# Layer 2's token sums taken from GpSimd to TensorE, with a newly searched instruction order

## Chip, core, metric

One core of a Trainium2 chip runs the whole kernel. The time is that of the core on the device, in microseconds (us); medians are given over several executions, with the range in brackets. The span, from the first to the last instruction in the trace, is 1.7 to 2.1 us shorter than the time in the profiled executions. Each execution also has a mean granted TensorE clock (1.0 is full speed). All comparisons are between executions that the records call fast; a single look has no state of its own, and is used where its clock is 1.0.

## The reference

Four layers work on x of 2048 tokens by 512, in bf16: linear attention, feed-forward, and both once more.

```python
def _A_ref(x, wqkv, wo):                  # layers 0 and 2; 32 heads of 16
    q, k, v = ...(x @ wqkv)...
    phi = lambda t: where(t > 0, t + 1, exp(t)) + 1e-6
    pq, pk = phi(q), phi(k)
    kv  = einsum("bhsd,bhse->bhde", pk, v)
    z   = einsum("bhsd->bhd", pk)         # the token sums of pk
    num = einsum("bhqd,bhde->bhqe", pq, kv)
    den = einsum("bhqd,bhd->bhq", pq, z)[..., None] + 1e-6
    return reshape(num / den) @ wo
def _B_ref(x, w1, w2):                    # layers 1 and 3; inner width 1376
    return maximum(x @ w1, 0) @ w2

x = x + _A_ref(_layernorm(x), ...)        # and so on: A, B, A, B
```

The change concerns z, the sum of pk over all 2048 tokens, in layer 2.

## The kernel before

The kernel builds a graph of small operations, each with its engine, what it reads and what it writes. A table, found beforehand by a search in a model of durations, gives the order in which they are issued; a second gives the bank, one of eight, of PSUM (the memory that holds TensorE's results) for each tile. Operations that may run on two engines carry an `a` (ScalarE) or `d` (VectorE) in the table. The tokens are 16 tiles of 128, in four chunks of four tiles.

For each tile, TensorE projects k, ScalarE and VectorE make pk of it, and in layer 2 (`zpn[0]` is 3) GpSimd adds the pk of the first three chunks into one f32 tile, which it splits into a high and a low bf16 half:

```python
def a_k_proj(i):
    b = alloc_bank()
    mm_group(... Tb[:, i, c, :], wqkv[:, c, D:2 * D] ...)           # 4 matmuls of N = 512
    phi_evac(b, pk_tile(i), ...)                 # ScalarE lin, exp; VectorE em (L515), phi (L517)
    if 0 < i < 4 * zpn[0]:
        prev = pk_tile(0) if i == 1 else zacc
        g.add(POOL, lambda e: e.tensor_tensor(zacc, prev, pk_tile(i), ALU.add), ...)     # L588
        if i == 4 * zpn[0] - 1:
            g.add(POOL, lambda e: e.tensor_copy(zhl[:, 0, :], zacc), ...)                # L591
            g.add(POOL, lambda e: e.tensor_tensor(zhl[:, 1, :], zacc, zhl[:, 0, :], ALU.subtract), ...)
```

What GpSimd hasn't summed goes to TensorE, as matmuls with a column of ones: pk is the weight side, so one of them is a weight load of 128x128 and a single column. The tiles and the two halves gather in one PSUM bank:

```python
def a_z_acc(lo, hi, zb, first):      # i < 0: one of the two halves
    return [(psv[:, zb, j:j + 1], src(i, j), ones[:, 0:1], ...)
            for i in range(lo, hi) for j in range(4)]
def tail_z():
    if zpn[0]:
        a_z_acc(-2, 0, zb, True)                                    # 8 matmuls of N = 1
    for k in range(zpn[0], NCH):
        a_z_acc(4 * k, 4 * k + 4, zb, k == 0)                       # 16 per chunk
```

Between layers the chunk's row statistics are small VectorE instructions of 128x4, with one power on GpSimd; then a tile pair is normalised and transposed by a DMA from SBUF to SBUF, whose result the next projection reads:

```python
def ln_chunk(t, first):              # L452 nm2, L454 var, L456 veps, L458 rstd, L460 nbias
    g.add(DVE,  ... nm2[:, sl] ...)
    g.add(DVE,  ... var[:, sl] ...)
    g.add(DVE,  ... veps[:, sl] ...)
    g.add(POOL, ... rstd[:, sl] = veps ** -0.5 ...)
    g.add(DVE,  ... nbias[:, sl] ...)
def tr_dma(lo, hi):
    dma(lambda e: e.dma_start_transpose(Tb[:, lo:hi], xn[:, lo:hi]), ..., 550.0 * (hi - lo), ...)
```

## Time and profile before

| | before |
|---|---|
| time, median of 3 | 277.51 us (277.36 to 278.38) |
| the execution that was profiled | 278.55 us, span 276.7, clock 1.0 |
| TensorE: 1893 matmuls, issue time | 263.4 us |
| TensorE: sum of its real stalls in that execution | 2.95 us |

The page's share of TensorE can't be used for fine readings, as the ends of matmuls are modelled. The issue time is worked out from starts instead, with the undisturbed steps that the prediction gives (216 ns for 128x512). A stall is what a start comes later than such a step. At a change to or from the tiled matmuls of the denominators the next start comes some 0.1 us later; these steps, and three others of 0.11 to 0.14 us, are left out of the 2.95 (the 0.19 at 176 us contains one).

One more line, from the page's list of DMA issues, for the transposes; the last number is the median from issue to landing.

```profile
Tb<-xn SPq DMA_TRANSPOSE x30, 3.2
```

### The profile page before, as it was taken

What the parts mean: (1) busy time and instruction counts of PE and PEld (TensorE: products, weight loads), DVE (VectorE), ACT (ScalarE), POOL (GpSimd) and SP (SyncE); (2) the same over time, 40 slices, a digit from 0 to 9 for tenths busy, and PEclk for the clock granted to TensorE, in tenths of its full rate; (3) what the DMA queues carried; (4) which work ended last, traced back from release to release, by engine and by line L of the source; (5) the groups of instructions that cost most, each with busy time, mean ns of one, the idle gap of its engine ahead of it and who ended that gap; (6) DMA issues with size and microseconds to landing.
All of it is one profiled execution on the core that took longest, in us unless ns stands there. A gap on an engine that the chain in (4) does not pass through costs nothing.

```text
span 276.7 us, 5086 instructions
## 1 busy us (share of the span) xinstructions
PE 268.8 (97%) x1893; PEld 162.4 (59%) x1893; DVE 239.6 (87%) x604; ACT 193.6 (70%) x423; POOL 33.3 (12%) x43
## 2 busy tenths in 40 slices
PE   6999999999999999999999999999999999999995
PEld 2444454434356766778756444344447777988884
DVE  4999789998995988499899978999999878899885
ACT  4898846998866179388678668589986958845510
POOL 3111000000201010001143481000012010100000
PEclk9999999999999999999999999999999999999999
DMA  6946960040413024201402130000340120600014
GB/s 207 378 97 100 264 202 0 0 78 19 77 32 65 0 40 91 45 19 27 52 0 42 39 73 2 0 2 14 64 95 2 38 57 12 165 19 2 1 76 154
DMA packets 41976, 18.35 MB, mean 66 GB/s; under 512 B 36352, under 2 KB 40544, under 8 KB 41952
## 3 DMA queue, kind: packets, MB, share of 16 engines
q1 hardware_dynamic: 41808, 17.96, 27.4%
q8 instruction: 15, 0.25, 0.4%
q14 instruction: 9, 0.07, 0.1%
q10 hardware_dynamic: 144, 0.07, 0.1%
HBM read 7.01 MB, written 2.10 MB: 33 GB/s over the span
## 4 chain that ended last, share of the span: by engine, by line
PE 81%; DVE 8%; DMA 8%; ACT 2%; issue 1%; SPq 0%
PE ps L531 81%; DMA Tb<-xn 4%; DMA w<-in_B_w_dram 2%; DVE big L517 1%; DMA xin<-in_A_x_dram 1%; DVE xres L575 1%; DVE bst L438 1%; DVE escr L515 1%; DVE xres L943 1%; ACT xn L468 1%; DVE xres L544 0%; DVE veps L456 0%; DVE nbias L460 0%; DVE xn L470 0%; DVE wper L785 0%
## 5 line engine op out<-in xcount | busy, mean ns | idle before, releaser
L513 ACT ACTIVATE escr<-ps 128x512 bf16<-128x512 f32 x64 | 37.8, 608 | 10.3 <-PE ps L531 9.5
L511 ACT ACTIVATE big<-ps 128x512 bf16<-128x512 f32 x64 | 37.7, 609 | 4.5 <-PE ps L531 4.4
L531 PE MATMUL ps<-Tb,w 128*128 128x512 bf16 x160 | 38.2, 379 | 0.0
L538 ACT ACTIVATE sqscr<-xres 128x512 bf16<-128x512 f32 x48 | 29.9, 628 | 6.4 <-DVE xres L575 6.0
L531 PE MATMUL ps<-wqkv,Tb 128*128 128x512 bf16 x128 | 30.8, 379 | 1.7 <-ACT rstd L1009 1.1
L531 PE MATMUL ps<-Tb,wqkv 128*128 128x512 bf16 x128 | 30.9, 379 | 0.5 <-DVE gw L621 0.5
L531 PE MATMUL ps<-gw,big 128*128 128x512 bf16 x128 | 31.4, 380 | 0.0
L531 PE MATMUL ps<-big,xn 128*128 128x512 bf16 x128 | 30.7, 379 | 0.0
L517 DVE TENSOR_TENSOR big<-big,escr 128x512 bf16<-128x512 bf16 x64 | 28.1, 462 | 0.9
L531 PE MATMUL ps<-w,xin 128*128 128x256 bf16 x190 | 26.3, 273 | 0.0
L564 POOL TENSOR_TENSOR rstdf<-varf,nhalf 128x4 f32<-128x4 f32 x8 | 8.5, 1072 | 138.9 <-DVE varf L562 53.2
L531 PEld LDWEIGHTS ps<-Tb,w 128*128 128x128 bf16 x160 | 15.1, 98 | 16.3 <-issue 0.5
L741 ACT ACTIVATE big<-ps 128x512 bf16<-128x512 f32 x34 | 19.7, 595 | 6.2 <-PE ps L531 6.1
L948 ACT ACTIVATE ps<-ps 128x256 f32<-128x256 f32 x28 | 10.5, 374 | 18.7 <-PE ps L531 16.4
L515 DVE TENSOR_SCALAR escr<-escr 128x512 bf16<-128x512 bf16 x64 | 19.4, 315 | 4.2 <-ACT escr L513 4.1
L531 PE MATMUL ps<-w2s,big 128*128 128x256 bf16 x160 | 21.9, 273 | 0.4 <-DVE xres L943 0.4
L531 PEld LDWEIGHTS ps<-wqkv,Tb 128*128 128x128 bf16 x128 | 12.1, 97 | 15.9 <-ACT rstd L1009 1.5
L865 ACT ACTIVATE big<-ps 128x512 bf16<-128x512 f32 (+1 forms) x33 | 16.8, 519 | 6.5 <-PE ps L531 6.2
L531 PE MATMUL ps<-w,big 128*128 128x256 bf16 (+2 forms) x113 | 21.1, 302 | 0.0
L531 PEld LDWEIGHTS ps<-Tb,wqkv 128*128 128x128 bf16 x128 | 12.0, 98 | 15.4 <-DVE gw L621 0.8
L531 PEld LDWEIGHTS ps<-w,xin 128*128 128x128 bf16 x190 | 18.5, 98 | 4.1 <-DVE xn L976 0.2
L531 PEld LDWEIGHTS ps<-big,xn 128*128 128x128 bf16 x128 | 12.2, 98 | 14.5 <-issue 0.5
(145 smaller groups left out, 494.1 us busy)
## 6 DMA issues: line engine op xcount, KB each, us to landing
wqkv<-in_A_wqkv_dram SPq DMA_DIRECT2D x3, 512.0 KB, 7.1
xin<-in_A_x_dram SPq DMA_DIRECT2D x3, 512.0 KB, 8.0
out_dram<-xn SPq DMA_DIRECT2D x3, 512.0 KB, 2.7
w<-in_B_w_dram SPq DMA_DIRECT2D x1, 1376.0 KB, 6.8
w<-in_B_w_dram SPq DMA_DIRECT2D x1, 1280.0 KB, 9.9
wo<-in_A_wo_dram SPq DMA_DIRECT2D x1, 512.0 KB, 10.0
Tb<-xn SPq DMA_TRANSPOSE x30, 3.2
xin<-in_A_x_dram SPq DMA_DIRECT2D x1, 384.0 KB, 3.2
```

The costliest lines, as they stand in the source:

```text
L438: g.add(DVE, lambda e: e.bn_stats(bst[:, i, :], xin[:, i, :]), [("xin", i)] + list(behind), [("bst", i)], C_DVE_BNST, name="bnst%d" % i)
L468: alts = [(ACT, lambda e: e.activation(xn[:, i, :], src, ACTF.Identity, scale=rstd[:, i:i + 1], bias=nbias[:, i:i + 1]), C_ACT_SB_AP), (DV ...
L511: g.add(ACT, lambda e: e.activation(dst_ap, psv[:, b, :], ACTF.Identity, bias=1.0 + 1e-6, scale=1.0), [("ps", b)], [dst_key], C_ACT_PSUM, ...
L513: g.add(ACT, lambda e: e.activation(escr[:, s, :], psv[:, b, :], ACTF.Exp), [("ps", b)], [("escr", s)], C_ACT_EXP, name=name + "_exp")
L515: g.add(DVE, lambda e: e.tensor_scalar(escr[:, s, :], escr[:, s, :], 1.0, 1e-6, ALU.min, ALU.add), [("escr", s)], [("escr", s)], C_DVE_BF4 ...
L517: g.add(DVE, lambda e: e.tensor_tensor(dst_ap, dst_ap, escr[:, s, :], ALU.max), [dst_key, ("escr", s)], [dst_key], 340.0, name=name + "_phi")
L531: last = e.matmul(o, l, r, start=st, stop=sp, skip_group_check=skip)
L538: g.add(ACT, lambda e: e.activation(sqscr[:, q, :], xres[:, i, :], ACTF.Square, accum_out=dst[:, i:i + 1]), [("xres", i)], [("sqscr", q), ...
L564: g.add(POOL, lambda e: e.tensor_tensor(rstdf[:, sl], varf[:, sl], nhalf[:, 0:4], ALU.pow), [("varf", t), ("nhalf",)], [("rstdf", t)], C_P ...
L741: g.add_flex([(ACT, lambda e, M=M, b=b, u=u: e.activation(unit_ap(u, M), psv[0:M, b, :], ACTF.Relu), C_ACT_PSUM), (DVE, lambda e, M=M, b=b ...
L865: g.add_flex([(ACT, lambda e: e.activation(out_ap(r, m), pv(b), ACTF.Relu), cost(C_ACT_PSUM)), (DVE, lambda e: e.tensor_scalar(out_ap(r, m ...
L948: g.add_flex([(ACT, lambda e: e.activation(psv[:, c1, cols], psv[:, c2, L], ACTF.Identity), 290.0), (DVE, lambda e: e.tensor_copy(psv[:, c ...
```

## The change

The intent is to take the f32 sums off GpSimd, where they block VectorE, and to give the search two truer durations: the transposes and the landing of the k weights (`wk`). Both tables are new. The diff, cut:

```diff
 ORDER = """
-17 0 14 12 15 18 13 1 16 19 2 20 22 3 24 4 21 23 25 5 6 26 27 7 28 8 29 40 30 33 31 32a ...
+17 0 14 12 15 18 13 1 16 19 2 20 22 3 24 4 21 23 25 5 6 26 27 7 28 8 29 33 30 47 31 32a ...
 ... (some 50 lines, all changed)
-BANKS = ("01435143526072607607676767706207072602266007067670720702760672...
+BANKS = ("01364701325424652425454545452625426426525564646246455426544262...
-... DEN_PRE=1, LATE_A=1, ZP=(0, 3), WK_ACT=False, ...
+... DEN_PRE=1, LATE_A=1, ZP=(0, 0), WK_ACT=False, ...
-        dma(... wqkv[:, :, D:2 * D] ..., 1650.0, "ld_wk", ...)
+        dma(... wqkv[:, :, D:2 * D] ..., 2000.0, "ld_wk", ...)
-                ... 550.0 * (hi - lo), "tr%d" % lo, issue=C_SP_TR)
+                ... 750.0 * (hi - lo), "tr%d" % lo, issue=C_SP_TR)
```

The two durations serve the model alone; on the chip they act only through the tables found with them.

## The prediction

> **What bounds the kernel now.** I read the page first (shares, then the chain), then TensorE's timeline, then VectorE's and GpSimd's timelines around the places where TensorE stood still, then the instructions of single lines.
>
> The engine shares and the chain that ended last:
>
> ```profile
> PE 268.8 (97%) x1893; PEld 162.4 (59%) x1893; DVE 239.6 (87%) x604; ACT 193.6 (70%) x423; POOL 33.3 (12%) x43
> ...
> PE 81%; DVE 8%; DMA 8%; ACT 2%; issue 1%; SPq 0%
> ```
>
> TensorE is the bound, and 97% says there is hardly any idle time to win. But ends of matmuls are modelled, so I counted from the starts. In undisturbed runs a 128x512 matmul starts 216 ns after the last, a 128x256 one 109, a 128x128 one 55 to 58, a 128x1 one 25. Summed over 1893 matmuls that is 263.4 us of issue. TensorE starts at 1.2 us and ends at 273.9; the remaining 9.0 us are 3.6 us of start-up (mostly waiting for the first weights and normalised tiles), some 2.5 us of small steps, most of them where TensorE changes to and from the tiled denominator matmuls, and six real stalls: 0.30 us at 37 us, 0.91 at 61.5, 0.59 at 143.8, 0.44 at 152.2, 0.19 at 176.1 and 0.52 at 179.6. They sum to 2.95 us, about 1.1% of the time. This is all that a better order can win outside the head and the tail.
>
> Two of the six, on TensorE's timeline where layer 1 hands over to layer 2:
>
> ```profile
> 143.10 1.03 PE L531 MATMUL ps<-wqkv,Tb 128*128 128x512 bf16 x4
> 144.55 1.26 PE L531 MATMUL ps<-w2s,big 128*128 128x256 bf16 x10 [0.42 <-DVE xres L943]
> ...
> 150.67 1.89 PE L531 MATMUL ps<-big,xn 128*128 128x512 bf16 x8
> 152.84 1.04 PE L531 MATMUL ps<-wqkv,Tb 128*128 128x512 bf16 x4 [0.28 <-DMA Tb<-xn]
> ```
>
> Four matmuls from 143.10 are issued by 143.96, yet the next starts at 144.55: 0.59. Eight from 150.67 are issued by 152.40, the next starts at 152.84: 0.44. Why VectorE was late there is on its own timeline, beside GpSimd's:
>
> ```profile
> 142.56 1.15 DVE L456 TENSOR_SCALAR veps<-var 128x4 f32<-128x4 f32 x1
> 145.39 1.27 DVE L517 TENSOR_TENSOR big<-big,escr 128x512 bf16<-128x512 bf16 x1
> 146.92 1.06 DVE L460 SCALAR_TENSOR_TENSOR nbias<-mean,rstd 128x4 f32<-128x4 f32 x1
> ...
> 142.54 1.16 POOL L588 TENSOR_TENSOR lden<-lden,big 128x512 f32<-128x512 f32 x1 [2.45 <-DVE var L454]
> 145.23 1.15 POOL L588 TENSOR_TENSOR lden<-lden,big 128x512 f32<-128x512 f32 x1 [0.42 <-DVE big L517]
> 146.81 1.15 POOL L588 TENSOR_TENSOR lden<-lden,big 128x512 f32<-128x512 f32 x1 [0.42 <-DVE big L517]
> ```
>
> A 128x4 instruction takes 1.15 us, and each long one ends when a GpSimd addition ends. All executions of these lines:
>
> ```profile
> L456 DVE TENSOR_SCALAR veps<-var x4: 170/170/1151, 102.4 to 153.8; 128x4 f32<-128x4 f32 x4
> L517 DVE TENSOR_TENSOR big<-big,escr x64: 407/419/1378, 11.0 to 197.7; 128x512 bf16<-128x512 bf16 x64
> ```
>
> Minimum, median, maximum: 0.17 against 1.15 us, 0.42 against 1.38. So the f32 sums cost VectorE, not GpSimd, and through it the two stalls.
>
> **What the Trainium skill says.** (1) "SBUF — State Buffer", section "SBUF: two separate sides": VectorE and GpSimd share one port pair, held for a whole instruction, and the loser "fully blocks". The trace agrees: VectorE's long instructions end with the 1.15 us addition. (2) "TensorE: Matmul & The Clock Gate", section "Back-to-back issue gap": an isolated matmul steps by N/2.4 + 2.5 ns, but in a stream of weight load and matmul both set the step. At N = 512 the trace has the formula's 216 ns; at N = 1 it has 25 ns, not 3, so the second half decides, and I use 25. (3) "Perfetto Trace Analysis", section "Identifying the Most-Contended Engine", warns against matmul busy time as a measure; here it shows 268.8 us where 263.4 is the issue.
>
> **The change part by part.**
>
> *Removed:* in layer 2 eleven additions, one copy and one subtraction on GpSimd, 11.9 + 1.2 + 0.6 + 1.2 = 14.9 us of an engine that is 12% busy. Worth nothing by itself. On VectorE it removes the blocking. Seven cases I can name: veps 1.15 for 0.17, nm 1.12 for 0.16, nbias 1.06 and 1.11 for 0.15, three L517 at 1.27, 1.27 and 1.38 for 0.42. Together 6.5 us of VectorE time between 142 and 162 us, where it is 94% busy. On the path that ends the kernel only what reached TensorE counts: 0.59 + 0.44 = 1.03 us.
>
> *Added:* chunks 0 to 2 of layer 2 (12 tiles, 4 matmuls each) go to the matmul with ones, 48 matmuls; the 8 on the two GpSimd halves go. Net 40. On TensorE's timeline:
>
> ```profile
> 170.98 0.34 PE L531 MATMUL ps<-ones,rhi 128*128 128x1 bf16 x8
> 171.18 0.54 PE L531 MATMUL ps<-ones,big 128*128 128x1 bf16 x16
> 171.58 1.02 PE L531 MATMUL ps<-big,xn 128*128 128x512 bf16 x4
> ```
>
> Starts 170.98, 171.18 and 171.58: 8 in 0.20 us, 16 in 0.40, thus 25 ns each. 40 x 25 = 1.0 us, fully on the bound engine. So removal and addition by themselves cancel: -1.03 + 1.00 = 0.
>
> *Moved:* the whole order is new, made with a transposed pair taking 0.75 us per tile instead of 0.55 and the first weights 0.35 us later. Fixed parts of the kernel's own model aside, that lengthens a pair by 0.4 us; the page has 3.2 us from issue to landing as the median of 30, and the chain shows that some are much longer:
>
> ```profile
> 57.90 4.63 DMA Tb<-xn
> ...
> 149.56 3.23 DMA Tb<-xn
> ```
>
> The 4.63 us one caused the largest stall, 0.91 us at 61.5. In the new order I counted TensorE work between the last matmul that feeds this transpose and the first that needs it: 6.8 us instead of 6.4, and the centring that precedes it moves ahead of the evictions. I expect 0.3 us to remain of 0.91. The stall at 37 us (sums waiting for pk of the last tiles) has one group of four 0.22 us matmuls put between in the new order; 0.1 of 0.30 remains. At 176 to 180 us, TensorE waits for the reciprocal chain and then for a PSUM bank that VectorE evicts after the last accumulation of G. The new order still lets 0.36 us of work stand between that accumulation and the first user of the bank, and the reciprocal has 3.0 us of TensorE work behind which to hide, while it took about 3.2 (two ScalarE passes of 0.69 and 0.63, a copy and a product of 0.42 and 0.75 on VectorE, plus gaps). So 0.5 of 0.71 stays. The head keeps its first projection at 7.2 us, since the first weights land at 7.0; nothing in the change makes them land earlier.
>
> Sum: stalls 2.95 - (0.3 + 0.1 + 0.5) = 2.05 us won, 1.0 us added, -1.05 net. A new order also makes new stalls; the old one left 1.9 us of stalls that no GpSimd sum explains, and a search with longer transposes should leave fewer. I allow 0.05 us beyond the 0.9 kept, little because the VectorE time won also helps other evictions: 277.5 - 1.05 + 0.05 = 276.5.
>
> **The rivals.** *A: only the added matmuls are felt.* The VectorE time won lies beside TensorE work, and the new order has its own stalls of the old size. Then 277.5 + 1.0 = 278.5 at most. For it: 268.8 of 276.7 us busy, and only 1.03 us of stalls are tied to GpSimd. Against it: both stalls are tied directly, link by link. *B: all stalls vanish.* 277.5 - 2.95 + 1.0 = 275.6; a shorter head or tail could take it to 275. For it: the search is told of the transposes that were too short. Against it: the G eviction has the same 0.36 us of cover. *C: a transpose becomes the new wait.* At the start of layer 2 the first transposed pair of chunk 2 has 10.8 us of TensorE work between producer and consumer, against 12.6 in the old order. Residuals, the row statistics with weight differences of 0.82 us put between them, the 1.03 us power, normalising and 3.2 us of transfer use some 10.5. A transfer of 4.6 us there would cost about 1.1 us: 277.6.
>
> **Range and chances.** The centre is 276.5. B bounds it below at 275.2 with a little from head and tail; C, or A in half, bounds it above at 277.9. A gain over 2% needs 272.0, less than the sum of issue, head and tail allows (even without any stall 275 or so): 0.01. A loss over 2% needs 283.1, five times the added matmuls; only a badly misjudged wait in the new order could do it: 0.02. Within 2%: 0.97.
>
> **What would show it right or wrong.** In the changed profile GpSimd should lose L588, L591 and L592, nothing else, and fall from 33.3 to about 18 us busy; L456, L452 and L460 should have maxima near 0.2 us and L517 near 0.45; 128x1 matmuls should number 128 and still step by 25 ns; the matmul issue should sum to 264.4. TensorE should show no wait on L943 or on a transpose between 138 and 155 us. The prediction is wrong if VectorE's long cases vanish but the stalls at the layer change persist (then the sums were not their cause), if a transpose wait over 0.5 us stands at the start of layer 2 (C), or if new stalls elsewhere sum to over 2 us.

## The result

The changed kernel takes 277.32 us (277.22 to 277.49, 4 runs) against 277.72 (277.36 to 278.38, 4 runs) of the kernel before in the same rounds. The ratio is 0.9983, with a 95% interval of 0.9962 to 1.0005. Ratios here are the mean time of one kernel's fast runs over that of the other's of the same rounds, so not quite the ratio of the medians quoted. The time is inside the range of 275.2 to 277.9, and "within 2%" was right. But the gain that was forecast, about 1.0 us, came out at 0.4 us by these medians and 0.17% (0.5 us) by the ratio; a repetition below gives 0.06 us. Where the rest went is the question.

The shares and the chain that ended last, of the changed kernel:

```profile
PE 268.6 (97%) x1909; PEld 164.2 (60%) x1933; DVE 236.8 (86%) x617; ACT 190.1 (69%) x410; POOL 18.3 (7%) x30
...
PE 94%; DVE 4%; issue 1%; ACT 0%; DVEq 0%
```

GpSimd has 13 instructions and 15 us less. DMA has left the chain, where it had 8%. 1933 weight loads are 40 more, as planned; the 1909 matmuls are fewer than the loads only because some records are missing (a second trace of this kernel, taken below, has all 1933).

Two of the lines that had been blocked, with minimum, median and maximum in ns:

```profile
L456 DVE TENSOR_SCALAR veps<-var x4: 164/170/171, 106.9 to 150.8; 128x4 f32<-128x4 f32 x4
```

```profile
L517 DVE TENSOR_TENSOR big<-big,escr x64: 409/424/428, 9.2 to 195.0; 128x512 bf16<-128x512 bf16 x64
```

The maxima were 1151 and 1378 ns; now no instruction of these lines is far from its median. TensorE's timeline at the hand-over from layer 1 to layer 2 (start in us, modelled duration, engine, line, operation, what, how many):

```profile
140.29 1.02 PE L531 MATMUL ps<-wqkv,Tb 128*128 128x512 bf16 x4
141.40 0.72 PE L531 MATMUL ps<-w2s,xin 128*128 128x256 bf16 x5
...
148.06 1.89 PE L531 MATMUL ps<-big,xn 128*128 128x512 bf16 x8
149.78 2.75 PE L531 MATMUL ps<-wqkv,Tb 128*128 128x512 bf16 x11
```

The first transposed chunk is used at 149.78 without a wait: eight matmuls from 148.06 at 0.216 us each end their issue at 149.79. The wait on a residual isn't quite gone: four from 140.29 are issued by 141.15, and the next starts 0.25 us later. The view names no cause for it; VectorE's timeline has two residual sums (L943) that end at 141.34, 0.06 us before that start. Further on, two waits persist, and there is a new one in the last layer:

```profile
178.36 0.40 PE L531 MATMUL ps<-rsp,esel 32*128 32x512 bf16 x4
179.14 2.12 PE L531 MATMUL ps<-Tb,wqkv 128*128 128x512 bf16 x9 [0.38 <-DVE gw L621]
```

```profile
266.23 0.71 PE L531 MATMUL ps<-w2s,big 128*128 128x256 bf16 x5
267.12 0.72 PE L531 MATMUL ps<-w2s,escr 128*128 128x256 bf16 x5 [0.18 <-DVE xres L943]
```

Five matmuls of 256 columns take 0.55 us to issue, so from 266.23 the next could start at 266.78, and starts 0.34 us later.

| TensorE's stalls, us, at | before, first profile | changed |
|---|---|---|
| 37 | 0.30 | 0 |
| 61 | 0.91 | 0 |
| 141 to 144 (residual) | 0.59 | 0.25 |
| 149 to 152 (transpose) | 0.44 | 0 |
| 176 to 180 | 0.19 + 0.52 | 0.17 + 0.44 |
| 267 | 0 | 0.34 |
| sum | 2.95 | 1.20 |
| issue time | 263.4 | 264.4 |

On this table the stalls fall by 1.75 and the issue rises by 1.0. The two traces' spans, 276.7 and 275.5, even fall by 1.2; the other 0.4 us lie mostly in the start-up and in the three small steps, which the new order doesn't have. This looks like the prediction come true, and it is deceptive: the first of the two executions was not a usual one.

### The profile page after: what moved, and what is told of

Same layout as the page of the kernel before. It is cut to its first block, busy times and chain, and to the rows that moved or that the text cites. A ratio compares the mean times of both kernels' runs of the same rounds, so it can differ in the third digit from the quotient of the medians.

```text
span 275.5 us, 5131 instructions
## 1 busy us (share of the span) xinstructions
PE 268.6 (97%) x1909; PEld 164.2 (60%) x1933; DVE 236.8 (86%) x617; ACT 190.1 (69%) x410; POOL 18.3 (7%) x30
## 4 chain that ended last, share of the span: by engine, by line
PE 94%; DVE 4%; issue 1%; ACT 0%; DVEq 0%
PE ps L531 92%; PE ps L415 2%; DVE xn L571 1%; DVE xres L575 1%; DVE xres L943 1%; PE ps L494 0%; DVE gw L621 0%; ACT Tb L501 0%; DVE xn L976 0%; DVE Tb L502 0%; DVE ps L949 0%; DVEq L1240 0%; DVE wrm L408 0%; ACT lnv L1007 0%
## 5 line engine op out<-in xcount | busy, mean ns | idle before, releaser
L531 PE MATMUL ps<-wqkv,Tb 128*128 128x512 bf16 x121 | 30.0, 379 | 0.7 <-DVE Tb L502 0.3
L531 PE MATMUL ps<-Tb,wqkv 128*128 128x512 bf16 x128 | 30.3, 379 | 0.4 <-DVE gw L621 0.4
L531 PE MATMUL ps<-gw,big 128*128 128x512 bf16 x118 | 29.4, 379 | 0.7 <-issue 0.2
L531 PE MATMUL ps<-big,xn 128*128 128x512 bf16 x123 | 29.7, 379 | 0.4 <-issue 0.2
L517 DVE TENSOR_TENSOR big<-big,escr 128x512 bf16<-128x512 bf16 x64 | 26.2, 423 | 2.9 <-ACT big L511 1.5
L515 DVE TENSOR_SCALAR escr<-escr 128x512 bf16<-128x512 bf16 x64 | 17.8, 289 | 9.8 <-ACT escr L513 9.4
L531 PEld LDWEIGHTS ps<-w,xin 128*128 128x128 bf16 x190 | 18.3, 98 | 4.7 <-DVE ps L949 0.3
L698 DVE TENSOR_TENSOR big<-big,ps 128x512 bf16<-128x512 bf16 x32 | 20.3, 682 | 0.4 <-PE ps L531 0.2
```

Of the source, the lines that this page charges most:

```text
L515: g.add(DVE, lambda e: e.tensor_scalar(escr[:, s, :], escr[:, s, :], 1.0, 1e-6, ALU.min, ALU.add), [("escr", s)], [("escr", s)], C_DVE_BF4 ...
L517: g.add(DVE, lambda e: e.tensor_tensor(dst_ap, dst_ap, escr[:, s, :], ALU.max), [dst_key, ("escr", s)], [dst_key], 340.0, name=name + "_phi")
L531: last = e.matmul(o, l, r, start=st, stop=sp, skip_group_check=skip)
L698: g.add(DVE, lambda e, j=j: e.tensor_tensor(unit_ap(us[j]), unit_ap(us[j]), psv[:, GB[j], :], ALU.mult), [("big", us[j]), ("ps", GB[j])], ...
```

## The experiments

My theory at this point, the first: (a) the end of the sums and the 40 matmuls each are worth 1.0 us and cancel; (b) the new order gains little or nothing, because the stall of 0.91 us at 61 us belongs to some executions and not to the order. The rivals, the second theory in its variants: the sums were worth more than the two stalls and the new order costs something; or the order gains about 1 us, and something unseen takes it back; or the 40 matmuls cost less or more than 25 ns each.

### Both kernels again

No edit.

> The kernel before, unchanged, profiled once more. Theory 1 (the profile that I predicted from was of a slow execution): that execution took 278.55 us while the other runs have a median near 277.5 us; time minus span was 1.82 us there and 1.74 us in the profiled run after, so a usual run before has a span of 275.7 to 275.9 us, and of the six stalls the one of 0.91 us behind the 4.63 us transpose is missing or below 0.2 us. Rival (the stall is the kernel's own): it is there again with over 0.7 us, the span is 276.5 us or more. The ratio to the kernel before should be 1.000 within 0.002 and tells the noise.

> The changed kernel, unchanged, for a narrower interval. Theory 1: ratio 0.9975 to 0.9990 (0.3 to 0.7 us faster), span 275.3 to 275.7 us. Rival (the gain of 1.2 us between the two profiled spans is real): ratio 0.9955 to 0.9965.

The kernel before took 277.25 to 277.56 us in its four fast runs (ratio 0.9989, 0.9959 to 1.0018, against the other runs of the same kernel). Its profile, at 313.83 us and clock 0.853, is not used. The changed kernel took 277.39 us (277.12 to 278.35, 6 runs) against 277.45 (277.3 to 279.65, 11 runs): ratio 0.9992, 0.9964 to 1.002. That is just outside what I expected of theory 1 (0.9975 to 0.9990). So the changed kernel is ahead by no more than the kernel before is of itself. Its second trace has no matmul record missing and repeats the first: the 40 added matmuls of one column step by 25 ns, which is the 1.0 us of issue, and the stalls are 0.25 at 141, 0.17 and 0.44 at 176 to 180, and 0.34 at 267.

### The sums alone, in the old order

The old tables stay, the eleven additions, the copy and the subtraction go, and the sums of chunks 0 to 2 stand where that of the halves stood.

```diff
-... ZP=(0, 3) ...
+... ZP=(0, 0) ...
 ORDER: old, without zp1 ... zp11, zhi, zlo
-... z-2 z12 ...
+... z0 z4 z8 z12 ...     (later numbers shifted)
```

> Old order, but the sums of layer 2 all on TensorE in the place where the two halves were summed, nothing on GpSimd. Theory 2 (the sums' removal pays for the 40 added matmuls): the stalls of 0.59 and 0.44 us at the hand-over to layer 2 vanish, 1.0 us is added, ratio 0.998 to 1.002. Rival (only the order search gained; VectorE's relief is hidden): stalls stay or come back as waits for the same transposes, ratio 1.003 to 1.004 (0.9 to 1.1 us slower).

It took 277.34 us (277.27 to 278.27, 6 runs), ratio 0.9997 (0.997 to 1.0023); the profiled execution took 277.32, span 275.6. TensorE's timeline in its hand-over:

```profile
141.91 1.03 PE L530 MATMUL ps<-wqkv,Tb 128*128 128x512 bf16 x4
142.78 1.25 PE L530 MATMUL ps<-w2s,big 128*128 128x256 bf16 x10
...
148.88 1.89 PE L530 MATMUL ps<-big,xn 128*128 128x512 bf16 x8
150.61 1.03 PE L530 MATMUL ps<-wqkv,Tb 128*128 128x512 bf16 x4
```

Four matmuls fill 0.87 us between 141.91 and 142.78, and eight fill 1.73 between 148.88 and 150.61: both stalls, 0.59 and 0.44, are gone without any new order. With the 40 matmuls in place the time equals that of the kernel before: the two cancel, as (a) says. (The interval alone would allow 0.8 us either way; that both parts are 1.0 us is read from the traces.) It also equals that of the changed kernel, 277.39 in the same rounds: the new order brought nothing that can be measured. Counted alike, with the small steps, the stalls of the two traces are 1.33 and 1.30 us: what the new order saves at 37 us and in the small steps it loses at 141 and 267. And in this trace, in the old order, there is no stall at 61 us: the transpose issued at 57.63 landed at 60.71.

### The 40 matmuls alone

The kernel before, with 40 needless matmuls with ones into unused columns, behind those of the halves.

```diff
-                        for i in range(lo, hi) for j in range(4)]
+                        for i in range(lo, hi) for j in range(4)] + (
+                    [(psv[:, zb, 8 + j:9 + j], src(-1, j % 4), ones[:, 0:1], False, False, True)
+                     for j in range(40)] if lo < 0 else [])
```

> The kernel before with 40 further 128x1 matmuls (into unused columns of the sums' bank, result unchanged) where the two halves are summed. Each should step by 25 ns, and nothing hides it: ratio 1.003 to 1.004 (0.9 to 1.1 us slower). Rival (VectorE or ScalarE is the true bound there and catches up behind them): under 0.4 us, ratio below 1.0015.

It took 279.2 us (278.47 to 281.4, 6 runs) against 277.66 (277.37 to 279.97, 11 runs): ratio 1.0057, 1.0016 to 1.0098. The median says 1.5, more than expected, but the executions differ much. Its two lowest are 278.47 and 278.49, the lowest of the kernel before in these rounds 277.37, 277.45 and 277.5: 1.0 us more, or 25 ns for each. The lowest of few runs are weak evidence by themselves; the trace has the same size:

```profile
172.51 1.34 PE L531 MATMUL ps<-ones,rhi 128*128 128x1 bf16 x48
173.71 0.54 PE L531 MATMUL ps<-ones,big 128*128 128x1 bf16 x16
```

Forty-eight matmuls fill 1.20 us, where eight had filled 0.20, and TensorE makes none of it good afterwards: against a usual execution (the fourth, below) it is 2.6 us late ahead of them, at 154.4, and 3.6 late behind them, at 182.9. The 2.6 us come from elsewhere. The profiled execution, at 281.14 and clock 0.994, had an extra wait where nothing was edited (the extra matmuls come after 170 us):

```profile
36.31 0.94 PE L531 MATMUL ps<-ones,big 128*128 128x1 bf16 x32
38.40 0.55 PE L531 MATMUL ps<-ones,big 128*128 128x1 bf16 x16 [1.15 <-DVE big L517]
```

VectorE was held there by the first feed-forward weights, which landed at 36.29 us instead of 35.45 in the first profile. The wait makes 1.0 us of the 2.6. The other 1.6 are the clock: the trace grants half of it from 38.99 to 42.40 us, where 128x512 matmuls start 427 ns apart instead of 216. Disturbances of about 1 us, from transfers, seemed possible in any execution, so I looked at them next.

### Further looks at the kernel before

No edit: three single profiles, on two chips.

> The kernel before once more, for a profile in the fast state (the last one fell in a slow execution). Theory 1 as before: span 275.5 to 275.8 us, the first transposes of layer 1 land in about 3.1 us each, no stall over 0.3 us near 61 us, the stalls of 0.59 and 0.44 us at the hand-over to layer 2 are there. Rival: the stall of 0.9 us near 61 us is there and the span is 276.5 us or more.

> The kernel before, for a profile of a usual execution: the last two executions of it that were profiled at full clock took 278.5 us, each with one transpose of over 4.6 us where TensorE has no cover (at 58 us in one, at 17 us in the other). Theory 1: in an execution of 277.3 to 277.7 us the span is 275.5 to 275.9 us, no transpose before 70 us takes over 4.2 us, TensorE has no stall over 0.35 us before 140 us (start-up aside), and the stalls of 0.59 and 0.44 us at the hand-over to layer 2 are there. If the execution is again of 278.2 us or more, one late transfer with a stall of about 0.9 us or more before 140 us. Rival: a usual span with a stall of 0.9 us, or a long span without one.

> The same as the run before it in this list, in case that one is slow: span 275.5 to 275.9 us without a stall over 0.35 us between the start-up and 140 us, or 276.5 us and more with one of about 0.9 us.

They took 278.50, 277.49 and 279.04 us, all at clock 1.0. The third, around 20 us on TensorE, and the transpose in its chain of waits (start, duration, what):

```profile
18.93 1.89 PE L531 MATMUL ps<-wqkv,Tb 128*128 128x512 bf16 x8
22.11 1.25 PE L531 MATMUL ps<-wqkv,Tb 128*128 128x512 bf16 x5 [1.30 <-DMA Tb<-xn]
```

```profile
17.24 4.83 DMA Tb<-xn
```

The fifth, at 62 us, and its transpose:

```profile
59.71 2.43 PE L531 MATMUL ps<-gw,big 128*128 128x512 bf16 x10
63.02 0.85 PE L531 MATMUL ps<-w,Tb 128*128 128x96 bf16 x16 [0.88 <-DMA Tb<-xn]
```

```profile
58.20 4.77 DMA Tb<-xn
```

The fourth, at the same place:

```profile
59.05 2.64 PE L531 MATMUL ps<-gw,big 128*128 128x512 bf16 x11 [0.19 <-issue]
61.53 0.84 PE L531 MATMUL ps<-w,Tb 128*128 128x96 bf16 x16
```

In the fourth nothing waits for a transpose there (eleven from 59.05 are issued by 61.43), and no transpose before 70 us took over 3.9 us. It is also the one that agrees with the median of 277.49 us of that call. So in three of the four usable traces of this kernel one transpose took 4.6 to 4.8 us instead of some 3.2; it was the one at 58, at 17 and at 58 us, and each of these executions was 1 us or more over the usual. (Another, at 128 to 130 us, takes 4.4 to 4.8 us in all four, but there nothing waits for it.)

The same matmuls can be set beside each other in the traces of this kernel. Against the fourth, TensorE in the first profile is 0.14 us late at 48 us, 1.05 at 62.6, and 1.07 at its last matmul. In the third it is 0.1 late at 18.5, 1.5 at 22.1, 1.05 at 38.5 (part is made good in the stall at 37, which is not there), and 1.02 at its last. In the fifth it is 0.44 late at 37.9, 1.49 at 63.0, 1.55 at its last. Thus one late transfer is nearly the whole of the first profile's difference from the usual execution, and little of it is regained later.

The usual execution, then, has these stalls: 0.37 at 37 us, 0.59 and 0.43 at the hand-over, and 0.19 and 0.52 at 175 to 179: 2.1 in all, not 2.95. With the three small steps (0.13, 0.14 and 0.14 us at 25, 59 and 233 us) it has 2.5; counted like this, the changed kernel has 1.3. Its two at the hand-over look as before:

```profile
142.04 1.03 PE L531 MATMUL ps<-wqkv,Tb 128*128 128x512 bf16 x4
143.50 1.26 PE L531 MATMUL ps<-w2s,big 128*128 128x256 bf16 x10 [0.43 <-DVE xres L943]
...
151.77 1.04 PE L531 MATMUL ps<-wqkv,Tb 128*128 128x512 bf16 x4 [0.27 <-DMA Tb<-xn]
```

How often does it happen? Of 45 fast executions of the kernel before, 12 took over 278.2 us, against 1 of 10 of the changed kernel and 2 of 6 of the sums alone in the old order. Most have no trace, so that each was a late transfer isn't shown; three of the 12, at 279.65 to 279.97, had the lower mean clock of 0.993 or 0.994 as well. Nor can it be said from ten runs whether the changed kernel is hit less often.

What makes a transpose late was in the traces, and I had missed it. The page lists, beside the kernel's own transfers (q1), packets whose kind it calls "instruction":

```profile
q8 instruction: 15, 0.25, 0.4%
```

Those of q8 are of 16 KB and take about 1 us. By the trace's table of packets, one starts at 60.47 in the first profile, at 20.06 in the third and at 60.93 in the fifth, each time while the late transpose is under way, and the last packet of the transpose ends 0.01 to 0.02 us after the end of that one. In the fourth the same two stand at 20.7 and 62.0, after the transposes of these places have landed (20.22 and 60.82). In the twelve traces at a clock of 0.99 or more there are 360 of these transposes. All 56 that took over 3.6 us overlap with an instruction packet of 8 or 16 KB; of the 248 that overlap with none the longest took 3.53. (Another 56 overlap and weren't late.) So each late transpose met such a packet. That this is what delays it is read from the traces; no run moved these packets, and why they come a microsecond earlier or later isn't known.

### The sums back on GpSimd, in the new order

The changed kernel with the additions put back, each right after its pk; the rest of the new order stays.

```diff
-... ZP=(0, 0) ...
+... ZP=(0, 3) ...
 ORDER: new; zp1 ... zp11, zhi, zlo added, each behind its pk
-... z0 z4 z8 z12 ...
+... z-2 z12 ...
```

> New order, but the sums of chunks 0 to 2 back on GpSimd, each addition right after its pk. Theory 2: VectorE's small instructions take over 1 us again in 3 or more cases near 145 to 152 us, TensorE gets 1.0 us less of matmuls and about 1 us of new stalls there; equal to the changed kernel within 0.6 us (ratio to before 0.996 to 1.001). Rival (VectorE's relief is hidden): 1.0 us faster than the changed kernel, ratio to before 0.994 to 0.9955.

It took 282.46 us (281.35 to 283.59, 6 runs), ratio 1.0171 (1.0136 to 1.0207), where I had expected the time of the changed kernel within 0.6 us. The median lies between two groups: three executions near 281.5 at clock 0.999 to 1.0, and three near 283.5 at 0.994, the profiled one among them. At the full clock that is 4 us slower than the kernel before, though it has the same work, and far more than the two stalls. GpSimd's timeline, then TensorE's:

```profile
152.83 3.62 POOL L588 TENSOR_TENSOR lden<-lden,big 128x512 f32<-128x512 f32 x3 [6.30 <-DVE big L517]
156.41 1.02 POOL L458 TENSOR_TENSOR rstd<-veps,nhalf 128x4 f32<-128x4 f32 x1
```

```profile
161.79 2.92 PE L531 MATMUL ps<-wqkv,Tb 128*128 128x512 bf16 x8 [2.89 <-DMA Tb<-xn]
164.51 1.73 PE L531 MATMUL ps<-big,xn 128*128 128x512 bf16 x4
```

The power of chunk 3's row statistics queues behind three additions, and with it the normalisation and the transpose: TensorE stands for 3.05 us at 158.5. Afterwards, from 162.52 to 165.93, the trace grants it half the clock, and its matmuls start 427 ns apart instead of 216, seven steps and part of an eighth: 1.6 us more, which goes with the 2 us between the two groups. Stalls of 0.49 us at 135.4, 0.70 at 141.0 and 0.2 to 0.5 at 148, 150 and 171 come on top.

### The same with the queue taken away

From this trace came a third theory: that the queue in front of chunk 3's power makes up most of the loss, which I took as 5 us, by the median. To tell the queue on GpSimd from the blocking of VectorE, the additions from the fourth on were put behind chunk 3's power.

```diff
 ORDER: as above
-... zp4 ... rstd3 ...
+... rstd3 zp4 ...
```

> New order with the sums on GpSimd again, as in the run that lost 5 us, but from the fourth addition on they stand behind the reciprocal root of chunk 3 in GpSimd's order. Theory 3 (the 5 us came from that root waiting behind three additions in GpSimd's own order, not from VectorE): the stall of 3 us before the transposes of chunk 3 vanishes, ratio to before 0.997 to 1.004. Rival (the shared port alone costs it): still over 1.010.

It took 280.75 us (280.65 to 281.12, 4 runs), ratio 1.0099 (1.0067 to 1.0131). My range was missed. All four are at clock 0.998 to 1.0, so they are to be held against the group at the full clock: there the queue explains about 1 of 4 us, and 3 remain. The half clock, which had cost the other group 2 us more, is in none of the four. What the 3 us are, VectorE shows, with GpSimd beside it:

```profile
153.07 0.99 DVE L460 SCALAR_TENSOR_TENSOR nbias<-mean,rstd 128x4 f32<-128x4 f32 x1
154.10 2.76 DVE L470 TENSOR_SCALAR xn<-xres,rstd,nbias 128x512 bf16<-128x512 f32 x2
```

```profile
152.89 4.98 POOL L588 TENSOR_TENSOR lden<-lden,big 128x512 f32<-128x512 f32 x4
```

Beside four additions, a 128x4 instruction takes 0.99 us for 0.16, and two normalisations 2.76 us, where the median of one is 0.545. TensorE now stands for 1.68 us at 158.1 and 1.17 at 162.4. The new order has 10.8 us of TensorE work between producer and consumer of chunk 2's transposes, against 12.6 in the old one. So with the sums placed in these two ways the new order can't hand over without a wait. The sums of the old order had been placed by a search and these were not, so it isn't shown that the new order could not carry them at all.

### Is there a version that beats both?

The largest stall that no transfer explains is the 0.52 us at 178 us: a fourth theory has it that TensorE waits for a PSUM bank that is evicted after the last accumulation of G. First, in the old order without sums, that accumulation is split into four groups, one for each bank, with bank 3 first, so that its eviction may begin earlier.

```diff
+            if i == NT - 1 and zpn[1]:           # layer 2 only
+                for c in (3, 0, 2, 1):
+                    mm_group(... one matmul, writes [("ps", GB[c])] ..., "gacc%d_%d" % (i, c))
+                return
```

> Old order with the sums on TensorE, and the last accumulation of G in layer 2 split into four matmuls with a semaphore each, the bank that the next projection needs first. Theory 4 (the 0.5 us stall after it is the eviction of that bank, which can start 0.65 us earlier): the stall goes below 0.15 us, span 275.0 to 275.2 us, ratio 0.9975 to 0.999. Rival (VectorE is behind there anyway): stall and span as in the unsplit run, 275.5 us.

It took 277.48 us (276.99 to 278.29, 6 runs), ratio 0.9986 (0.9956 to 1.0017). In the sums alone the wait was this:

```profile
179.16 1.90 PE L530 MATMUL ps<-Tb,wqkv 128*128 128x512 bf16 x8 [0.46 <-DVE gw L620]
```

and with the split this:

```profile
178.93 1.90 PE L530 MATMUL ps<-Tb,wqkv 128*128 128x512 bf16 x8 [0.16 <-DVE gw L626]
```

From the starts, the stall fell from 0.52 to 0.23, and the lowest execution's span from 275.5 to 275.2. That is the right direction and a smaller step than expected, and too little to be seen in the medians.

Then the rest of that stall and the one at 37 us were attacked as well: the eviction of bank 3 ahead of a VectorE product, and the last sums of layer 0 behind one accumulation.

```diff
 ORDER, layer 2
-... u0_2 ... gev3d ...
+... gev3d u0_2 ...
 ORDER, layer 0
-... z12 gacc11 gacc12 ...
+... gacc11 z12 gacc12 ...
```

> The split run's kernel, with the eviction of the bank that the next projection needs put ahead of a product on VectorE in layer 2, and the last group of sums in layer 0 moved behind one accumulation. Theory 4: stalls of 0.30 us at 37 us and 0.23 us at 178 us go, the second to under 0.1; undisturbed executions at 276.5 to 276.8 us (277.0 before this), ratio 0.996 to 0.998. Rival: the reciprocal chain or the matrix after it waits instead (a new stall of 0.2 to 0.6 us at 39 or 181 us), ratio 0.998 to 1.000.

It took 277.68 us (276.7 to 278.24, 6 runs), ratio 0.9988 (0.9956 to 1.0021). In the trace the stall at 178 us is gone. The one at 37 us is still there with 0.25 us (four matmuls from 37.16 are issued by 38.03, the sums start at 38.27), and another has come:

```profile
42.57 1.89 PE L530 MATMUL ps<-Tb,wqkv 128*128 128x512 bf16 x8
45.15 0.39 PE L530 MATMUL ps<-rsp,esel 32*128 32x512 bf16 x4 [0.69 <-DVE gw L626]
```

Eight matmuls from 42.57 are issued by 44.30; the next waits 0.85 us, for VectorE, whose two evictions of G ended at 45.09. In the split's trace they ended at 44.29, and nothing waited. As far as the traces show, those 0.8 us come from late transfers and not from the order: the feed-forward weights, which VectorE works on in between, landed at 36.16 and 39.84 us here and at 35.25 and 39.04 there. This is the trap once more: the profiled execution took 277.59, and the two lowest, which have no trace, 276.70 and 276.73, just what was expected of undisturbed ones and the lowest of all. What the reordering at 37 us is worth thus isn't shown. Neither this version nor the split is faster than the kernels before and after within the intervals.

## Why the prediction was right or wrong

**The sums and the 40 matmuls: right, and to size.** Removal was put at 1.03 us and the matmuls at 1.00. The sums alone in the old order took away just the two stalls, and gave the same time; 40 matmuls alone added 1.0 in undisturbed executions. The links in between hold too: GpSimd 18.3 us busy, 40 more weight loads, 1.0 us more of issue, maxima of 171 and 428 ns. One line was read too neatly: of the three long VectorE instructions shown, two end within 0.02 us of an addition, but the one at 145.39 ends 0.28 us after it. And the page of the Trainium skill cited for the 25 ns has that figure itself, as the least step of short matmuls; no second cause from the weight loads was needed.

**"I expect 0.3 us to remain of 0.91": this is the step that failed.** That TensorE waited for a transpose of 4.63 us was read rightly. But the sum counted 0.6 us as won against a base that never had it. The base was 277.5, the median; the stall was in an execution of 278.55. In the usual execution (277.49) the stall is 0, and the old order without sums had none there either. So that term of the sum is 0, not 0.61: the largest part of the 0.8 us that were missed.

**"I allow 0.05 us" for new stalls: too little, and the second step that failed.** The changed kernel has 0.25 us left at 141 and 0.34 new at 267, in both of its traces: 0.59. The allowance was a hope about searches, not a reading. (For the first I had said there would be no wait on a residual between 138 and 155 us.)

**The small terms.** At 37 us 0.37 was won in place of 0.2, and 0.4 in the small steps, where the prediction had expected nothing. At 176 to 180 us 0.61 stayed in place of 0.5.

With the usual execution as base the sum closes: stalls 2.5 less 1.3 is 1.2 won, 1.0 added, so about 0.2 us gained. The spans say the same, 275.7 against 275.5. The prediction of 276.5 was 0.8 us low.

**The rivals.** A, that only the matmuls are felt, is ruled out: the time didn't rise by 1.0. B, that all stalls vanish, as well. C was half right: a late transpose costs about 1 us, but in the order before as it stands, in places that change from run to run; at the start of layer 2 of the new order none was seen in its two traces. A late transpose met an instruction packet each time; no run here varied when these come, so that this is the cause rests on the traces alone.

**The searched order** gained nothing that could be measured beyond what removing the sums does in the old order. The additions put back into it, in two placements, cost 3 to 4 us at the full clock.

## What to carry to other kernels

Before stalls are counted from a trace, compare that execution's time with the median of the others, and its clock too: a stall that the usual execution doesn't have can't be won, and two traces can differ by as much as the gain that is looked for. When work goes from one engine to another, do that alone in the old order first; here it showed that a blocking of 1.03 us had been exchanged for 1.0 us of issue on the bound engine. And an order found by a search holds for the contention it was found with; putting back a little work on an idle engine can cost several times what it cost in the old one.

## What the Trainium skill lacked or had wrong

- "TensorE: Matmul & The Clock Gate", section "Part 1: The HAM clock gate": its table has the clock fall after one idle window or more of some 3.4 us. Here a stall of 3.05 us was followed by steps of 427 instead of 216 ns (its own half-clock figure, 426.7, agrees); the trace has them from 0.7 us after work had resumed, for 3.4 us. In another kernel a stall of 1.29 us was followed, 0.6 us later, by 3.4 us at half the clock. Three of the six executions of the first kernel had the lower mean clock of 0.994, with times near 283.5 against 281.5 us. The page says that the window runs freely and that frequent short idle times can bring the clock down; a single stall shorter than the window isn't among its cases. (A stall of 1.46 us in the third profile had no such effect.)
- The same page, section "Back-to-back issue gap": it puts the spacing in a stream of weight loads and matmuls at some 81 ns for 128 columns and 131 for 512, and says that the formula for isolated matmuls fits neither. Here, with a weight load for each of 1893 matmuls, the steps are 56 and 216 ns, those of the formula. For one column the trace has 25 ns, which is the page's own floor.
- "DMA: Bandwidth & Descriptors", section "Latency and other measured facts": there is a bandwidth for DMA transposes, but neither a latency from SBUF to SBUF nor its spread. Here a pair of tiles takes 3.2 us in the median, and now and then the same instruction takes 4.63, 4.77 or 4.83 us in another execution. The section names no case in which one comes late; here all 56 that took over 3.6 us overlap with an instruction packet.
- No page that I found says that a profiled execution should be held against the median of the unprofiled ones. Here three of four usable profiles of one kernel were 1.0 to 1.6 us over its usual time, each with one late transfer.
